# An MLP stage in another order: loads, the first token tile and the transposes rearranged

## The chip, the cores and the metric

The kernel runs on one core of a Trainium2 chip. The metric is the device time of one execution in microseconds (us). A profile of one execution gives a span from the first to the last instruction, 1.7 to 2.3 us shorter than that time in the runs here. Engines: PE is TensorE (PEld its weight loads), DVE is VectorE, ACT is ScalarE, POOL is GpSimd, SP is SyncE, which issues the DMAs. "Clock" is the TensorE clock that was granted, as a share of full speed.

## The reference

A layer norm of x (2048 tokens, 640 features) feeds two branches that are added to x: linear attention with 32 heads, and an MLP of width 1536. The MLP stage below is its first product with the gelu.

```python
xn = _layernorm(x)
return x + _A_ref(xn, A_wqkv, A_wo) + _B_ref(xn, B_w1, B_b1, B_w2, B_b2)
# _B_ref: h = gelu(xn @ w1 + b1);  h @ w2 + b2
```

## The kernel before

Tokens come in 16 tiles of 128. Each is normalized on DVE with token rows on partitions. The first MLP product needs it transposed (`xnT`), either by five PE transposes and a copy from PSUM on DVE, or by a DMA transpose issued on SP. W1 comes in four pieces of three unit columns each (`JQ = 3`, twelve units in all).

```python
dma_x(0, 1); b1 load; dma_w1(0); dma_x(1, 1); dma_w1(1); dma_x(2, 1)   # condensed
dma_w1(2); dma_x(3, 1); dma_w1(3); then x4-7, x8-11, x12-15
TD = 6                                     # tiles from 6 on are transposed by DMA
...
def h_unit(t0, n, jb):                     # one unit: 5 matmuls of n*128 columns, one gelu
    b = take(1)
    Pl.ins("tensor", [... matmul(bank(b, 0, w), W1[:, k, jb...], xnT[:, k, tok]) for k in range(DT)],
           reads=[r_W1[...]] + r_xnT[t0:t0 + n], writes=[B_[b]])
    Pl.ins("scalar", ... ACT.Gelu_apprx_tanh ...)
...
def ln_aggr(t):                            # mean and variance on DVE, then rstd on POOL
    Pl.ins(v, ... bn_aggr ...)
    Pl.ins(g, ... veps = var + EPS ...)
    Pl.ins(g, ... rstd = veps ** -0.5 ...)
def ln_norm(t):                            # on DVE, needs aggr and rstd
    ...
```

A planner writes each engine's instructions in program order and adds a wait wherever a value comes from another engine or a DMA. An instruction that waits therefore holds everything behind it on its engine. In the stage with DMA transposes the kernel before normalizes tile t - 1 after the statistics of tile t, puts one weight load after every second transpose, and two mask instructions on POOL after each tile.

## Time and profile before

| What | Value |
|---|---|
| time, median of 3 executions | 219.55 us (219.39 to 219.61) |
| span of the profiled execution | 217.9 us, clock 1.00 |
| PE busy | 208.8 us, 96% |
| first MLP matmul / first K matmul (end of the MLP stage) | 7.41 us / 64.97 us |
| waits of PE in that stage | 1.3 us for the copy of tile 1, 1.6 us for the DMA transpose of tile 11 |

How to read it: PE is nearly always busy, so the time is PE's work plus its gaps. All the work behind the MLP stage is a fixed chain, 217.9 - 64.97 = 152.9 us long. What counts is when the MLP stage ends.

This is the view of busy time in given stretches, for the kernel before; the columns are the stretch, its length, busy us and instructions of PE, PEld, DVE, ACT and POOL, then clock, DMA share and GB/s.

```profile
9.50:12.50 3.00, 1.70 (x28) 1.53 (x29) 2.44 (x7) 0.92 (x4) 0.97 (x3) 1.00 1.08 346
12.50:15.50 3.00, 3.00 (x38) 2.76 (x36) 1.86 (x6) 2.40 (x7) 0.61 (x2) 1.00 1.07 362
```

PE waits in the first stretch, and works at full clock in the second.

### The profile page before, as it was taken

The page shows a single profiled execution, that of the slowest core. Times are in us where ns is not written, and L with a number is a line of the kernel's source. Part 1 is how long each engine was busy: PE and PEld are TensorE (multiplying, and loading weights), DVE is VectorE, ACT ScalarE, POOL GpSimd, SP SyncE. Part 2 cuts the span into 40 slices and gives each one's busy share as a digit, 9 for nine tenths or more (in the row PEclk, how much of TensorE's full clock was granted, in tenths as well). Part 3 has the DMA queues.
Part 4 walks back from the last instruction along what each step waited for, and adds up shares of the span by engine and source line. Part 5 has one row for each costly group of instructions (what it writes and reads, how often), then busy time and mean ns, then how long its engine had stood idle before and what let it go on. Part 6 is the DMA issues. An engine that isn't in the chain of part 4 may idle for free.

```text
span 217.9 us, 3898 instructions
## 1 busy us (share of the span) xinstructions
PE 208.8 (96%) x1592; PEld 142.3 (65%) x1592; DVE 122.0 (56%) x217; ACT 74.2 (34%) x140; POOL 41.7 (19%) x74
## 2 busy tenths in 40 slices
PE   7799998899999999999999799999999999999994
PEld 2489987444447777777666555667767776777772
DVE  2765997000005888899168679989739316712211
ACT  2378988466667555111253653400000000000000
POOL 2221798000000000000000000099991000000000
PEclk9999999999999999999999999999999999999999
DMA  5990289995000000000000000344500110000011
GB/s 149 339 353 8 35 220 240 293 312 200 3 0 0 0 3 0 0 3 0 0 3 0 2 3 0 120 127 136 191 33 30 48 45 30 30 30 33 30 55 37
DMA packets 20425, 17.12 MB, mean 79 GB/s; under 512 B 7352, under 2 KB 20408, under 8 KB 20408
## 3 DMA queue, kind: packets, MB, share of 16 engines
q1 hardware_dynamic: 20408, 16.88, 26.2%
q8 instruction: 12, 0.20, 0.4%
q14 instruction: 5, 0.04, 0.1%
HBM read 12.62 MB, written 2.62 MB: 70 GB/s over the span
## 4 chain that ended last, share of the span: by engine, by line
PE 74%; DVE 16%; DMA 5%; SPq 1%; issue 1%; ACT 0%; DVEq 0%
PE ps L577 34%; PE ps L352 16%; PE ps L464 10%; PE ps L453 10%; DVE PQ L443 5%; DVE stats L309 4%; DMA xPK<-in_A_x_dram 3%; DMA xnT<-xn_tm 3%; PE ps L533 2%; DVE ek L441 2%; DVE rden L538 2%; DVE xn_tm L329 1%; DVE PQ L540 1%; SPq L235 1%; DVE aggr L314 1%
## 5 line engine op out<-in xcount | busy, mean ns | idle before, releaser
L352 PE MATMUL ps<-xnT,W 128*128 128x128 bf16 (+2 forms) x450 | 53.5, 280 | 3.2 <-DMA xnT<-xn_tm 1.6
L577 PE MATMUL ps<-W,HG 128*128 128x320 bf16 x384 | 54.9, 299 | 0.3 <-DVE PQ L443 0.3
L352 PEld LDWEIGHTS ps<-xnT,W 128*128 128x128 bf16 x450 | 36.3, 98 | 19.5 <-issue 2.5
L577 PEld LDWEIGHTS ps<-W,HG 128*128 128x128 bf16 x384 | 37.5, 98 | 15.7 <-issue 0.7
L356 ACT ACTIVATE HG<-ps,b1c 128x128 bf16<-128x128 f32 (+2 forms) x90 | 41.0, 489 | 17.7 <-PE ps L352 15.8
L549 POOL TENSOR_TENSOR xnT<-xnT,b2bc 128x640 bf16<-128x640 bf16 x16 | 22.6, 1451 | 104.0 <-DMA xnT<-in_A_x_dram 104.0
L440 ACT ACTIVATE ek<-ps 128x512 bf16<-128x512 f32 (+1 forms) x36 | 23.2, 645 | 23.7 <-PE ps L453 9.2
L441 DVE TENSOR_SCALAR ek<-ek 128x512 bf16<-128x512 bf16 (+1 forms) x36 | 10.9, 304 | 36.2 <-ACT ek L440 35.1
L583 DVE TENSOR_TENSOR out_sb<-ps,xnT 128x640 bf16<-128x640 f32 x15 | 12.3, 822 | 33.5 <-PE ps L577 31.5
L577 PE MATMUL ps<-Msb,PQ 128*128 128x320 bf16 x160 | 24.5, 299 | 0.0
L486 PE MATMUL ps<-xnT,Wqkv 128*128 128x512 bf16 x100 | 22.1, 379 | 0.0
L453 PE MATMUL ps<-Wqkv,xnT 128*128 128x320 bf16 x160 | 21.9, 299 | 0.0
L464 PE MATMUL ps<-xPK,xn_tm 128*128 128x320 bf16 x160 | 21.9, 299 | 0.0
L453 PEld LDWEIGHTS ps<-Wqkv,xnT 128*128 128x128 bf16 x160 | 15.7, 98 | 6.2
L464 PEld LDWEIGHTS ps<-xPK,xn_tm 128*128 128x128 bf16 x160 | 15.7, 98 | 6.1
L577 PEld LDWEIGHTS ps<-Msb,PQ 128*128 128x128 bf16 x160 | 15.7, 98 | 6.1
L309 DVE BATCH_NORM_STATS2 stats<-xPK 128x6 f32<-128x320 bf16 x32 | 15.6, 486 | 4.8 <-DMA xPK<-in_A_x_dram 4.4
L486 PEld LDWEIGHTS ps<-xnT,Wqkv 128*128 128x128 bf16 x100 | 11.7, 117 | 9.5
L443 DVE SCALAR_TENSOR_TENSOR PQ<-ps,ek 128x512 bf16<-128x512 f32 x20 | 13.8, 692 | 2.1
L443 DVE SCALAR_TENSOR_TENSOR xPK<-ps,ek 128x640 bf16<-128x640 f32 x16 | 13.2, 825 | 1.7
L538 DVE RECIPROCAL rden<-den_sb 128x512 bf16<-128x512 f32 x4 | 13.4, 3353 | 0.1
L540 DVE TENSOR_TENSOR PQ<-PQ,rden 128x512 bf16<-128x512 bf16 x20 | 12.2, 675 | 0.1
(50 smaller groups left out, 94.3 us busy)
## 6 DMA issues: line engine op xcount, KB each, us to landing
xnT<-in_A_x_dram SPq DMA_DIRECT2D x4, 640.0 KB, 4.1
Wqkv<-in_A_wqkv_dram SPq DMA_DIRECT2D x3, 800.0 KB, 6.6
out_dram<-out_sb SPq DMA_DIRECT2D x15, 160.0 KB, 1.8
W<-in_B_w_dram SPq DMA_DIRECT2D x4, 480.0 KB, 5.6
xPK<-in_A_x_dram SPq DMA_DIRECT2D x3, 640.0 KB, 8.5
W<-in_B_w_dram SPq DMA_DIRECT2D x1, 1920.0 KB, 10.1
Wo<-in_A_wo_dram SPq DMA_DIRECT2D x1, 800.0 KB, 5.5
xPK<-in_A_x_dram SPq DMA_DIRECT2D x4, 160.0 KB, 4.7
```

What stands on the lines that cost most here:

```text
L309: Pl.ins(v, lambda e: e.bn_stats(stats[:, s, 6 * h:6 * h + 6], x_in[:, t, h * HW:(h + 1) * HW]), reads=[r_x[t]], writes=[r_stats[s]])
L352: Pl.ins("tensor", [(lambda e, k=k: e.matmul(bank(b, 0, w), W1[:, k, jb * P:(jb + 1) * P], xnT[:, k, tok], start=(k == 0), stop=(k == DT - ...
L356: Pl.ins("scalar", lambda e: e.activation(HG[:, jb, tok], bank(b, 0, w), ACT.Gelu_apprx_tanh, bias=b1c[:, jb:jb + 1]), reads=[B_[b], r_b1c ...
L440: Pl.ins("scalar", lambda e: e.activation(e2, src, ACT.Exp), reads=br, writes=[r_ek[s]])
L441: Pl.ins(v, lambda e: e.tensor_scalar(et, et, 1.0, 1e-6, ALU.min, ALU.add), reads=[r_ek[s]], writes=[r_ek[s]])
L443: Pl.ins(v, lambda e: e.scalar_tensor_tensor(out=d2, in0=src, scalar=0.0, in1=e2, op0=ALU.max, op1=ALU.add), reads=br + [r_ek[s]], writes= ...
L453: fns.append(lambda e, k=k, h=h, b=b, t=t: e.matmul(bank(b + h, 0, HW), xnT[:, k, t * P:(t + 1) * P], Wqkv[:, k, D + h * HW:D + (h + 1) * ...
L464: Pl.ins("tensor", [(lambda e, t=t, h=h, b=b, f=f: e.matmul(bank(b + h, 0, HW), xn_tm[:, t, f * P:(f + 1) * P], PK[:, t, h * HW:(h + 1) * ...
L486: Pl.ins("tensor", [(lambda e, k=k, j=j, b=b: e.matmul(bank(b), Wqkv[:, k, j:D:DT], xnT[:, k, cc], start=(k == 0), stop=(k == DT - 1))) fo ...
L538: Pl.ins(v, lambda e: e.reciprocal(rden[:], den_sb[:]), reads=[r_den], writes=[r_rden])
L549: Pl.ins(g, lambda e: e.tensor_tensor(out=x_res[:, t, :], in0=x_res[:, t, :], in1=b2bc[:], op=ALU.add), reads=[r_xr[t // CH], r_b2], write ...
L577: return lambda e: e.matmul(bank(b + h, 0, HW), seq[i][0], seq[i][1][:, h * HW:(h + 1) * HW], start=(i == 0), stop=(i == n - 1))
```

## The change

The intent is to start PE earlier and to take its two waits away. Tile 0 goes in two column pieces, so that the first matmuls start on two fifths of it. Tiles 1 to 3 go through PE and all later ones through DMA, with no weight load between the transposes. x1 is loaded ahead of W1, W1's last piece ahead of x3, and b1 from ACT. The masks come at the end.

```diff
         dma_x(0, 1)
-        dma_w("sync", b1tmp[:], ...)
+        dma_x(1, 1)
         dma_w1(0)
-        dma_x(1, 1)
         dma_w1(1)
         dma_x(2, 1)
         dma_w1(2)
+        dma_w1(3)
         dma_x(3, 1)
-        dma_w1(3)
-        for c in range(1, NC):
+        dma_x(4, 2)
+        dma_x(6, 2)
+        for c in range(2, NC):
             dma_x(c * CH, CH)
 ...
+        ln_stats(0)
+        ln_half(1, 0); ln_half(1, 1); ln_aggr(1)
+        norm0(0, CA, r_xnA); norm0(CA, D, r_xnB)      # two pieces of tile 0
+        dA, sA, bA = transp0(0, 2, r_xnA)
+        filler(1)
+        dB, sB, bB = transp0(2, DT, r_xnB)             # copies: first on DVE, second on ACT
+        b1_step(); ln_norm(1); ln_half(2, 0)
+        h_first([0, 1, 2])
+        TD = 4
+        def pe_tile(t):
+            b = transp(t)
+            xnT_copy(t, b)
+            ln_half(t + 1, 1)
+            ln_aggr(t + 1)
+            ln_half(t + 2, 0)
+            ln_norm(t + 1)
+        pe_tile(1)
+        units(0, 1, 3, 2 * JQ)
+        units(1, 1, 0, 3)
+        pe_tile(2)
+        units(1, 1, 3, 2 * JQ)
+        units(0, 2, 2 * JQ, 3 * JQ)
+        pe_tile(3)
+        units(0, 2, 3 * JQ, JT)
+        for t in range(TD, NT):
+            if t > TD:
+                ln_norm(t)
+            ... dma_start_transpose(tile t) ...
+            if t + 1 < NT: ln_half(t + 1, 1); ln_aggr(t + 1)
+            if t + 2 < NT: ln_half(t + 2, 0)
+        Pl.records["sync"] += late                     # all late weights
+        run_masks(len(mask_jobs))
+        for (t0, n) in [(2, 1), (3, 1), (4, 2), (6, 2), (8, 4), (12, 4)]:
+            units(t0, n, 0, JT)
```

## The prediction

> **What bounds the kernel now.** I read the page first, then the waits of PE, the timeline of the first 40 us on all engines, the chain that ended last, and the landing time of single DMA issues.
>
> ```profile
> PE 208.8 (96%) x1592; PEld 142.3 (65%) x1592; DVE 122.0 (56%) x217; ACT 74.2 (34%) x140; POOL 41.7 (19%) x74
> ...
> PE   7799998899999999999999799999999999999994
> ```
>
> TensorE is busy for 96% of the 217.9 us span. The second line (40 slices) has two dips before the middle: the start, and slice 7 near 38 us. So an MLP reorder can win only idle time of PE, matmuls that vanish, or an earlier start. The waits of PE up to 72 us (total, times, longest) are small:
>
> ```profile
> PE ps L352 <- DMA xnT<-xn_tm: 1.6, 1, 1.6
> PE ps L352 <- DVE xnT L344: 1.6, 2, 1.3
> ```
>
> L352 is the first MLP matmul. The wait of 1.3 us is here in the timeline:
>
> ```profile
> 9.49 0.45 PE L336 MATMUL ps<-ident,xn_tm 128*128 128x128 bf16 x5 [0.24 <-DVE xn_tm L329]
> ...
> 10.29 0.49 DVE L309 BATCH_NORM_STATS2 stats<-xPK 128x6 f32<-128x320 bf16 x1 [0.22 <-DMA xPK<-in_A_x_dram]
> ...
> 10.71 0.47 DVE L344 COPY xnT<-ps 128x640 bf16<-128x640 bf16 x1
> ...
> 11.24 2.39 PE L352 MATMUL ps<-xnT,W 128*128 128x128 bf16 x35 [1.30 <-DVE xnT L344]
> ```
>
> The transposes of tile 1 are ready near 9.9, but VectorE, in program order, stands at the statistics of tile 3, whose x lands only at 10.24; the copy out of PSUM queues behind. The other wait is in the chain (start, us, what):
>
> ```profile
> 13.91 2.18 PE ps L352 x20
> ...
> 18.59 2.23 PE ps L352 x40
> ...
> 32.96 5.71 DMA xnT<-xn_tm
> 38.67 0.25 issue
> 38.91 26.06 PE ps L352 x120
> 64.97 21.73 PE ps L453 x160
> ```
>
> The transpose of tile 11 took 5.7 us because weight loads of 800 KB stand between the transposes; the first two, on an empty queue, took 2.9 and 2.6 us. The MLP ends at 64.97 and what follows is not touched: any change of that moment moves the end by as much. The same lines give the matmul pitch: 2.18/20 = 109 ns for 256 columns, 2.23/40 = 55.8 ns for 128, 26.06/120 = 217 ns for 512. A unit of five matmuls is thus 0.279, 0.545 or 1.086 us for one, two or four tiles.
>
> **What the Trainium skill says.** "TensorE: Matmul & The Clock Gate", section "Wait — 56ns, not 53.3ns?", gives a warm pitch of N/2.4 GHz plus 2.5 ns, 55.8 ns at 128 columns; the trace agrees. "DMA: Bandwidth & Descriptors", section "Queues, rings and completion order", says that each DMA engine consumes descriptors in ring order but that completion is not FIFO. Here the seven early loads did land in issue order (x0 3.1, W1 piece 0 5.9, x1 6.4, piece 1 7.8, x2 8.3, piece 2 9.8, x3 10.24), then the last W1 piece, issued at 4.85 and landed 6.9 us later:
>
> ```profile
> W<-in_B_w_dram SPq DMA_DIRECT2D x1, 480.0 KB, 6.9
> ```
>
> Section "Issuing engines are not separate DMA queues" of that page says that another issuing engine saves only sequencer time. So moving b1 to ScalarE brings no bandwidth; nothing before is issued there, so no trace shows it yet.
>
> **The change part by part.**
>
> *Loads.* x1 goes ahead of W1 piece 0, and W1 piece 3 ahead of x3. Bytes ahead of and with x1 fall from 0.80 to 0.32 MB: it lands near 3.6 to 4.0. But x3 now lands where the last W1 piece landed before, 4.85 + 6.9 = 11.75 at the latest; 0.25 us earlier if x1 fills part of the hole between 2.5 and 4.0 us, where the DMA moved only 84 to 124 GB/s. I take 11.5, against 10.24 before. This is the term on which the rest hangs.
>
> *Tile 0.* Both halves of tile 1's statistics stand ahead of tile 0's normalization, but that costs nothing: it waited 1.09 us for the rstd from POOL anyway. The first piece (256 columns) starts at 5.45 as before, is transposed near 5.9 and copied by VectorE near 6.3; the second follows a filler and goes through ScalarE, whose gelus took 0.37, 0.47 and 0.69 us for 128, 256 and 512 columns, so about 0.58 us for 384. Second half ready near 7.4. Three units are then done near 7.9, against 7.41 + 0.84 = 8.25: 0.3 us won here.
>
> *Tile 1.* Its copy no longer stands behind the statistics of tile 3, so the 1.3 us wait goes: its units run near 9.4, not 11.24.
>
> *Tile 2, the new wait.* The order on VectorE is copy of tile 1, second half of tile 2, its aggregate, first half of tile 3, and only then the normalization of tile 2. It therefore stands behind x3. PE has only six units and three more of tile 1 up to the transposes of tile 2, done near 10.3. They start at x3 + 0.42 (pitch from statistics to the next operation, 10.29 to 10.71) + 0.45 (normalization) + 0.1 = P = 12.47. So PE waits about 2.2 us here, and everything won at tiles 0 and 1 is absorbed. From P on:
>
> - transposes 0.28, three units of tile 1 0.84, three pair units 1.64: P + 2.76.
> - tile 3's normalization waits for its rstd. From an aggregate's start to the normalization it feeds is 1.30 us (4.15 to 5.45). Copy of tile 2 at P + 0.41, statistics 0.80, aggregate 1.33, normalization 2.61, done 3.06: PE starts at P + 3.10, so it waits 0.35.
> - transposes 0.28 and three pair units 1.64: P + 5.02.
> - 24 units of tiles 2 and 3 at 0.279 = 6.70: P + 11.72.
> - 24 pair units at 0.545 = 13.08: P + 24.80.
> - 24 four-tile units 26.06: P + 50.86 = 63.3.
>
> Two tiles fewer on PE are in that: 2 x 0.28 = 0.56 us. Masks at the end leave POOL's chain of veps and rstd undisturbed; before, VectorE had two stages of slack, now the loop normalizes right after the aggregate of the same tile with one half statistic between. Before, a tile took 1.53 us:
>
> ```profile
> 25.21 0.21 DVE L314 BATCH_NORM_AGGREGATE aggr<-stats 128x2 f32<-128x12 f32 x1
> ...
> 25.34 0.44 DVE L329 TENSOR_SCALAR xn_tm<-xPK,aggr,rstd 128x640 bf16<-128x640 bf16 x1
> ...
> 25.70 1.01 DVE L309 BATCH_NORM_STATS2 stats<-xPK 128x6 f32<-128x320 bf16 x2
> ```
>
> Now it takes normalization 0.36, half 0.53, aggregate to the next normalization 1.28: 2.17 us, slower, but it begins earlier: tile 4 at P + 5.71 = 18.2 (23.85 was the first by DMA, tile 6). With 0.5 to the issue and 2.6 to 2.9 to the landing, tile 5 is there at P + 11.1, needed at 11.72; tile 11 at P + 24.0 to 24.3, needed at 24.80; tile 15 near 45.5, needed near 50. So the 1.64 us wait at 38 goes, with about half a microsecond to spare. The weights start near 43 instead of 27: 2.4 MB of Wqkv at the 330 to 370 GB/s seen takes 7 us and is wanted at 63; b2, Wo and W2 follow by 58.
>
> The sum: 64.97 - 63.3 = 1.6 us earlier, which follows from -1.3 (tile 1) - 1.64 (tile 11) - 0.56 (transposes) - 0.3 (tile 0) + 2.2 + 0.35 (new waits) = -1.3, the difference being 0.3 us of small gaps before. 219.55 - 1.6 = 217.9.
>
> **Rivals.**
>
> *The x3 wait does not come.* If VectorE were past tile 3's statistics before PE runs dry, P would be 10.3 and the MLP would end near 61.2: 215.8. For it speaks the intent of the change; against it, the landing times, which are set by bytes, and the strict order of VectorE seen at 10.29.
>
> *The slower loop on VectorE becomes the bound.* 0.1 us more per tile uses 0.7 us by tile 11 and the margin is gone; 0.3 us more per tile costs about 1.5 us, and the time returns to 219.4. For it speaks the thin margin; against it, that POOL is freed of masks, which took 0.2 to 0.5 us each between its rstd steps.
>
> *The late weights become the wait.* They would have to take more than 20 us for what took under 17 when interleaved with transposes. I give this little; it would put the time above 220.
>
> *The b1 load behind other traffic* holds the in-order PE before its first units. A wait of under 4 us vanishes in the x3 wait.
>
> **Range and chances.** The centre is 217.9. The early end is x3 at 11.0 and smaller gaps (about 217.0), and a little for the first rival: 216.6. The late end is a used-up margin or x3 at 12.2: 219.2. Faster by 2% needs 215.16, below even the full first rival (215.8): 5%. Slower by 2% needs 223.9, where only the weights or b1 could bring it: 2%.
>
> **What would show it.** In the changed profile: PE idle for about 2 us before the transposes of tile 2, near 10.3 to 12.5, with VectorE's idle before the first half of tile 3 put down to the x DMA, and this longer than any wait for the copy out of PSUM. Transposes on DMA landing in under 3 us, at a pitch of about 2.2 us, with "POOL rstd" as what ended VectorE's idle in each. No wait of PE near 37. K stage starting near 63.3. I am wrong if PE runs through 10 to 13 us without a gap (then the time is below 217), or if the DMA wait at tile 4 or 8 is over 1 us (then it is 219 or more).

## The result

The changed kernel takes 221.03 us (median of 4: 220.35, 221.28, 221.28, 220.79), the kernel before 219.47 us in the same rounds (4 executions). The ratio is 1.0066, 95% interval 1.004 to 1.0092. Ratios here are the mean time of one kernel's fast runs over that of the other's of the same rounds, so not quite the ratio of the medians. That is within 2% of before, but slower beyond noise where 1.6 us faster was forecast, and outside the range of 216.6 to 219.2. The profiled execution is the fastest of the four (220.35 us); what made the others up to 0.9 us longer was not traced.

The page of the changed kernel (its slowest stretches are seen in the clock row, 40 slices of 5.5 us each):

```profile
PE 208.5 (95%) x1572; PEld 142.6 (65%) x1581; DVE 120.7 (55%) x216; ACT 74.7 (34%) x141; POOL 42.1 (19%) x74
...
PEclk9969999999999999999999999999999999999999
```

PE has two tiles of transposes fewer (a few other records are missing from both traces), yet is busy almost as long as before. The clock row has a 6, which it had nowhere before. The waits of PE from 7 to 66 us (total, times, longest):

```profile
PE ps L336 <- DVE xn_tm L329: 2.4, 1, 2.4
PE ps L352 <- issue: 1.1, 1, 1.1
```

L336 is the transpose of a tile on PE, L352 an MLP matmul. Both waits of the kernel before are gone, and two others have come. The first is the forecast one (the timeline of the first 48 us, all engines: start, us, engine, line, operation, and in brackets the idle time before it and what ended it):

```profile
11.61 0.49 DVE L309 BATCH_NORM_STATS2 stats<-xPK 128x6 f32<-128x320 bf16 x1 [1.91 <-DMA xPK<-in_A_x_dram]
12.02 0.43 DVE L329 TENSOR_SCALAR xn_tm<-xPK,aggr,rstd 128x640 bf16<-128x640 bf16 x1
...
12.51 0.71 PE L336 MATMUL ps<-ident,xn_tm 128*128 128x128 bf16 x5 [2.38 <-DVE xn_tm L329]
```

DVE stands at tile 3's statistics until x3 lands, 1.3 us later than before; only then may it normalize tile 2. PE is idle for 2.38 us. What was not forecast is what follows (the chain that ended last):

```profile
13.22 3.62 PE ps L352 x30
16.84 0.28 PE ps L336 x5
17.12 8.34 PE ps L352 x135
25.46 1.09 issue
26.55 13.26 PE ps L352 x120
...
65.71 21.73 PE ps L474 x160
```

The 30 matmuls of the first line are three units of one tile and three of two, 0.84 + 1.64 = 2.48 us at the pitches of before; they took 3.62. The stretches say why:

```profile
9.50:12.50 3.00, 0.62 (x12) 0.45 (x9) 1.04 (x3) 0.93 (x3) 0.79 (x2) 0.93 1.08 351
12.50:15.50 3.00, 2.99 (x25) 2.75 (x26) 1.50 (x5) 1.10 (x3) 0.79 (x2) 0.50 1.07 363
```

From 12.5 to 15.5 us PE is busy all the time, but at a clock of 0.50, and does 25 matmuls where the kernel before did 38 (in both a mix of 128 and 256 columns). The edges of the fall are seen in half-us stretches:

```profile
12.00:12.50 0.50, 0.00 (x0) 0.00 (x0) 0.45 (x2) 0.00 (x0) 0.00 (x0) 0.56 1.07 364
15.00:15.50 0.50, 0.50 (x5) 0.34 (x3) 0.04 (x1) 0.23 (x1) 0.36 (x1) 0.52 1.05 358
```

They read 0.56 and 0.52, so the clock was halved from about 12.06 to 15.48, for 3.4 us.

The other wait, "1.09 issue" at 25.46, has no name in the chain. Tile 4 and tile 5 must both have landed there. These are the DMA transposes of tile 4 (issued at 19.84) and of tile 5 (issued at 22.00), with the us from issue to landing last, from the view of DMA issues:

```profile
xnT<-xn_tm SPq DMA_TRANSPOSE x1, 2.6
xnT<-xn_tm SPq DMA_TRANSPOSE x1, 4.5
```

22.00 + 4.5 = 26.5: it is tile 5 that PE waits for. Its data moved from 23.0 to 24.2 us, as one would expect, and in the last of that time another queue appears (DMA queues from 24.0 to 24.5 us: packets, MB, share of 16 engines):

```profile
q8 instruction: 1, 0.02, 13.9%
```

13.9% of 16 engines for half a us is 1.1 us of one engine, for one packet. The only other transpose that took over 3.0 us was tile 11's, 4.2 us, issued at 34.98, with the next packet of that queue at 36.9. The other ten took 2.6 to 3.0.

In sum the MLP stage ends at 65.71 instead of 64.97, and 218.6 - 65.71 = 152.9 us follow, exactly as before.

### The profile page after: what moved, and what is told of

Read it like the earlier page. It is cut to its first block, busy times and chain, and to the rows that moved or that the text cites. A ratio compares the mean times of both kernels' runs of the same rounds, so it can differ in the third digit from the quotient of the medians.

```text
span 218.6 us, 3880 instructions
## 1 busy us (share of the span) xinstructions
PE 208.5 (95%) x1572; PEld 142.6 (65%) x1581; DVE 120.7 (55%) x216; ACT 74.7 (34%) x141; POOL 42.1 (19%) x74
## 4 chain that ended last, share of the span: by engine, by line
PE 83%; DVE 9%; DMA 3%; issue 2%; SPq 2%; DVEq 0%
PE ps L598 34%; PE ps L352 23%; PE ps L474 10%; PE ps L485 10%; DVE PQ L464 3%; DMA xPK<-in_A_x_dram 3%; PE ps L507 2%; PE ps L554 2%; DVE rden L559 2%; SPq L235 1%; DVE ek L462 1%; DVE PQ L561 1%; DVE W L531 1%; SPq L231 1%; DVE ZB L521 1%
## 5 line engine op out<-in xcount | busy, mean ns | idle before, releaser
L352 PE MATMUL ps<-xnT,W 128*128 128x128 bf16 (+2 forms) x432 | 53.3, 286 | 1.5 <-issue 1.1
L352 PEld LDWEIGHTS ps<-xnT,W 128*128 128x128 bf16 x435 | 36.6, 100 | 17.5 <-issue 1.2
L356 ACT ACTIVATE HG<-ps,b1c 128x128 bf16<-128x128 f32 (+2 forms) x87 | 40.3, 493 | 17.8 <-PE ps L352 15.9
L598 PE MATMUL ps<-Msb,PQ 128*128 128x320 bf16 x160 | 24.5, 299 | 0.0
L507 PE MATMUL ps<-xnT,Wqkv 128*128 128x512 bf16 x97 | 21.6, 379 | 0.2
L309 DVE BATCH_NORM_STATS2 stats<-xPK 128x6 f32<-128x320 bf16 x32 | 15.0, 469 | 5.0 <-DMA xPK<-in_A_x_dram 4.9
## 6 DMA issues: line engine op xcount, KB each, us to landing
W<-in_B_w_dram SPq DMA_DIRECT2D x1, 1920.0 KB, 15.5
```

The source lines that it names most:

```text
L309: Pl.ins(v, lambda e: e.bn_stats(stats[:, s, 6 * h:6 * h + 6], x_in[:, t, h * HW:(h + 1) * HW]), reads=[r_x[t]], writes=[r_stats[s]])
L352: Pl.ins("tensor", [(lambda e, k=k: e.matmul(bank(b, 0, w), W1[:, k, jb * P:(jb + 1) * P], xnT[:, k, tok], start=(k == 0), stop=(k == DT - ...
L356: Pl.ins("scalar", lambda e: e.activation(HG[:, jb, tok], bank(b, 0, w), ACT.Gelu_apprx_tanh, bias=b1c[:, jb:jb + 1]), reads=[B_[b], r_b1c ...
L507: Pl.ins("tensor", [(lambda e, k=k, j=j, b=b: e.matmul(bank(b), Wqkv[:, k, j:D:DT], xnT[:, k, cc], start=(k == 0), stop=(k == DT - 1))) fo ...
L598: return lambda e: e.matmul(bank(b + h, 0, HW), seq[i][0], seq[i][1][:, h * HW:(h + 1) * HW], start=(i == 0), stop=(i == n - 1))
```

## The experiments

Twelve kernels ran in three lots of four. The kernel before had medians of 219.59, 219.52 and 219.57 us. Its executions were at clock 1.00, except one (221.24 us) and three (221.41 to 221.52), which had a mean clock of 0.992. No trace of those exists, so where their clock fell is open. They count in the ratios, so I compare medians and give the ratio where it is needed.

### 1. x3 loaded ahead of the last W1 piece

```diff
-        dma_w1(3)
         dma_x(3, 1)
+        dma_w1(3)
```

> The changed kernel with x3 loaded ahead of the last W1 piece again. Theory (x3 sets tile 2, its wait lets the clock fall): x3 lands near 10.2 instead of 11.6, PE idles about 1 us before the transposes of tile 2 instead of 2.4, the granted clock stays at 1.0, the transposes start near 11.1, and the MLP ends between 62.0 and 63.5 instead of 65.7: 216.6 to 218.2 us. Rival (the slower DMA-transpose loop bounds the stage): tile 5 lands when it did, the wait moves there, and the time stays within 0.5 us of 221.0.

Measured: 218.74 us, ratio 0.9973 (0.995 to 0.9996), clock 1.0 in all four executions. That is 2.3 us less than the changed kernel, but above the 216.6 to 218.2 that I expected. PE's timeline:

```profile
11.54 0.45 PE L336 MATMUL ps<-ident,xn_tm 128*128 128x128 bf16 x5 [1.16 <-DVE xn_tm L329]
...
24.77 39.16 PE L352 MATMUL ps<-xnT,W 128*128 128x256 bf16 x237 [1.24 <-issue]
```

The gap before tile 2 is 1.16 us and the clock does not fall. The tile-2 part of the theory holds. The end, 63.9 us, is later than expected (62.0 to 63.5), because the wait for tile 5 stands: its transpose took 4.6 us again. So the rival was right about the second wait, though that wait is not a matter of DVE's loop alone, as experiment 5 shows.

### 2. The gap filled with empty matmuls

`filler(n)` issues n matmuls of 512 columns on a tile of zeros.

```diff
+        filler(9)
         pe_tile(2)
```

> The changed kernel with nine matmuls on the zero tile ahead of the transposes of tile 2, so that PE is busy for 1.9 of the 2.4 us in which it waits for x3; x3 and tile 2 come no earlier. Theory (the idle stretch costs twice, because the clock halves after it): granted clock 1.0 from 12 to 15.5 us, tile 2's transposes start at 12.5 as before, and the time falls by 1.0 to 1.5 us to about 219.7. Rival (the clock in the record is a symptom without cost, or falls at that time whatever PE does): no change, 221.0.

Measured: 220.16 us (219.49 to 220.22), ratio 1.0025, clock 1.0 in all four. Tile 2's transposes start at 12.77, no earlier than in the changed kernel. The 30 matmuls behind take 2.64 us in the timeline, where 3.83 were needed at the half clock, so the fall of the clock costs 1.2 us there. But only 0.9 us reached the end, a little less than the 1.0 to 1.5 expected:

```profile
12.77 0.45 PE L336 MATMUL ps<-ident,xn_tm 128*128 128x128 bf16 x5 [0.56 <-DVE xn_tm L329]
...
26.36 39.16 PE L352 MATMUL ps<-xnT,W 128*128 128x256 bf16 x237 [1.60 <-issue]
```

PE comes to tile 4 earlier and waits longer for tile 5, whose transpose took 5.0 us. In the profiled execution the MLP stage ends only 0.2 us earlier than the changed kernel's. The half clock is avoidable, and is a cost of its own; the wait behind it takes back part of what is won.

### 3. PE given other work ahead of tile 2

```diff
-        units(1, 1, 0, 3)
-        pe_tile(2)
-        units(1, 1, 3, 2 * JQ)
+        units(1, 1, 0, 2 * JQ)
         units(0, 2, 2 * JQ, 3 * JQ)
+        pe_tile(2)
+        units(0, 2, 3 * JQ, JT)
+        units(2, 1, 0, 5)
         pe_tile(3)
-        units(0, 2, 3 * JQ, JT)
+        units(2, 1, 5, JT)
```

> The changed kernel with PE's order alone changed: the last three units of tile 1 and three pair units go ahead of the transposes of tile 2, five units of tile 2 ahead of those of tile 3. Same loads, same order on VectorE. Theory (PE waits for x3 only because it has nothing else in its order): no gap at 10 to 12.5 us, no fall of the clock; but tile 5 then lands 2 us or more after PE is through with tile 3 (near 21.5), since VectorE's chain starts no earlier, so a wait of 2 to 4 us appears there, perhaps with the clock falling; MLP ends at 62.5 to 64.5, 217.2 to 219.2 us. Rival (the chain on VectorE was not near the bound): no wait at tile 4, MLP ends near 61, 215.7 us.

Measured: 219.81 us (219.57 to 219.93), clock 0.992 in all four: 0.6 us above the range that I gave. PE runs without a gap from 9.5 to 22 us, as expected. Then it stands at the pair of tiles 4 and 5 (tile 5 landed last, at 24.21), and the clock falls there instead:

```profile
24.30 40.83 PE L352 MATMUL ps<-xnT,W 128*128 128x256 bf16 x237 [2.34 <-DMA xnT<-xn_tm]
```

In the one-us stretches from 24 to 28 the clock is 0.66, 0.50, 0.50 and 0.63. The gap of 2.4 us had moved by 12 us, and took its halved clock along. Both costs belong to the gap, not to that moment of the kernel; and what PE wins by filling one gap it loses in the next if DVE's chain of normalizations starts no earlier.

### 4. The new order of loads alone, in the kernel before

```diff
         dma_x(0, 1)
         b1 load
+        dma_x(1, 1)
         dma_w1(0)
-        dma_x(1, 1)
         dma_w1(1)
         dma_x(2, 1)
         dma_w1(2)
-        dma_x(3, 1)
         dma_w1(3)
+        dma_x(3, 1); dma_x(4, 2); dma_x(6, 2)
```

> The kernel before with the new order of loads alone (x1 ahead of W1 piece 0, W1 piece 3 ahead of x3, x4 to x7 in two loads; b1 stays on SyncE). Theory: x3 at 11.6 holds the copy of tile 1 on VectorE until 12.0, PE idles 2.7 us or more from about 9.5 and the clock halves after it: 1.3 to 3 us slower than the kernel before, 220.8 to 222.5. Rival (the order of the loads is not what costs): within 0.4 us of 219.5.

Measured: 222.76 us (221.32 to 223.74), ratio 1.0145 (1.0099 to 1.019): 3.2 us slower than the kernel before, the largest effect of all, and a little beyond my range.

```profile
12.98 3.99 PE L354 MATMUL ps<-xnT,W 128*128 128x128 bf16 x35 [3.02 <-DVE xnT L346]
```

The 1.3 us wait of before has become 3.0, and 35 matmuls that took 2.39 us then take 3.99 now. The mean clock of the four executions was 0.992, 0.992, 0.985 and 0.999; the one at 0.999 is the fastest, 1.2 to 2.4 us ahead of the others. So the order of the loads is the part of the change that costs, and much of that cost is the clock.

### 5. The instruction packet moved

PE's matmuls and weight loads are 1592 + 1592 instructions in the kernel before, and its instruction queue q8 moved 12 packets of 0.20 MB together. The Trainium skill, "Runtime: NRT & Kernel Launch", section "Instruction fetch mechanics", says that an engine's instruction memory is refilled in blocks of 16 KiB, 256 instructions, through a DMA queue of its own. 3184 / 256 is 12.4, an estimate from the page's block size that counts no waits or branches: the packets of q8 fit PE's own instructions. If so, more PE instructions at the start move a packet to an earlier time, without a change elsewhere.

```diff
-        filler(10)                     # 10 matmuls of 512 columns on the zero tile
+        (42 matmuls of 128 columns on the zero tile)
```

> The changed kernel with its first ten zero matmuls of 512 columns replaced by 42 of 128 columns: the same stretch of time, but 64 more PE instructions, so what PE fetches after a fixed number of instructions comes about 1.8 us earlier. Theory (the transposes that share their data time with a 16 KB packet of the instruction queue land 2 us late): the packet moves from 24.0 to about 22.2, between the data of tiles 4 and 5; tile 5 lands in 2.6 to 3.0 us instead of 4.5, no wait at 25.5 us, MLP ends about 64.6, 219.9 us. Rival (the second transpose is late for a reason of its own): tile 5 takes 4.5 us again, 221.0.

Measured: 219.38 us (218.28 to 219.81). The packet came at 22.5 instead of 24.0, just after the data of tile 4. It was through at 23.7, when those of tile 5 (from 23.4) had just begun. The queue moved 13 packets in the whole execution instead of 12. The transpose of tile 5, issued at 22.37, landed in 2.9 us:

```profile
xnT<-xn_tm SPq DMA_TRANSPOSE x1, 2.9
```

This is PE's timeline behind tile 3's transposes:

```profile
17.33 47.50 PE L352 MATMUL ps<-xnT,W 128*128 128x256 bf16 x375
```

One unbroken line up to the end of the stage: the wait is gone, though PE's gap before tile 2 is still 2.39 us and the clock still fell in three of the four executions. The fourth, at 0.999, took 218.28 us, near the 217.9 that I had forecast.

> Both: x3 ahead of the last W1 piece, and the 42 narrow matmuls in place of the ten wide ones. Theory: the packet moves from 22.05 to about 20.3, tile 5 lands near 22.8 instead of 24.7, the 1.24 us wait at 23.5 goes, MLP ends near 62.7, 217.5 us. Rival: as with x3 ahead alone, 218.7.

With x3 ahead as well: 217.11 us (216.84 to 217.87), ratio 0.9887, clock 1.0 throughout, 1.6 us less than x3 ahead alone. It was run at another time. Tile 5 landed in 3.1 us, although the packet (20.4 to 21.3) still reached into the first 0.4 us of its data, and the same unbroken line appears:

```profile
14.73 47.50 PE L352 MATMUL ps<-xnT,W 128*128 128x256 bf16 x375
```

The rival (the second transpose is always late) falls in both. In the seven traces looked at with this loop on a queue without loads (the changed kernel, experiments 1, 2, 3, both of 5, and 7), every transpose that took over 3.5 us, from 4.0 to 5.0, had a packet of q8 in its data time or at its end: tile 5 or, where the packet came earlier, tile 4 (4.0 us in experiment 3), and a later one, tile 9 or 11. But not every transpose that met a packet was late: besides tile 5 here, two took only 3.3 and 3.4. In the traces of experiments 8 and 9 one transpose took 3.7 us although its packet ended 0.1 us after its issue. Why the packet holds up a transpose by about 2 us, when its own time is 1.1 us, these traces do not show.

### 6. Weights between the transposes again

```diff
             ... dma_start_transpose(tile t) ...
+            if t % 2 and late:
+                Pl.records["sync"].append(late.pop(0))
```

> The changed kernel with the late weights put between the transposes again, one load after every odd tile, as in the kernel before. Theory (the emptied queue removed the wait for tile 11): transposes behind 800 KB land in 4 to 7 us, tile 11 issued near 35 lands near 40.5 to 41.5 and PE waits 0.7 to 1.7 us for it near 40: about 222. Rival (the margin is there anyway): no such wait, 221.0.

Measured: 221.16 us (220.96 to 221.73), no different from the changed kernel by the median, and below the 222 expected. In the profile the expected wait is there:

```profile
40.17 26.06 PE L352 MATMUL ps<-xnT,W 128*128 128x512 bf16 x120 [0.83 <-DMA xnT<-xn_tm]
```

Transposes behind a large load took 3.1 to 5.6 us. So the emptied queue does remove 0.8 us of wait in this execution. It can't be read from the medians alone, since the clock falls in some executions and not in others: 220.96 and 220.97 at 1.000, 221.73 and 221.36 at 0.992. In the profiled execution the gap before tile 2 was 2.42 us, and the clock did not fall.

### 7. Masks between the tiles again

```diff
             if t + 2 < NT:
                 ln_half(t + 2, 0)
+            run_masks(2)
```

> The changed kernel with two mask instructions after each tile's part of the DMA-transpose loop. Theory: POOL is idle 1.29 us per tile in that loop and the two masks take about 0.8, so they fit: loop pitch stays 2.16 us, within 0.4 us of 221.0. Rival (masks at the end are what keeps the rstd chain short): pitch over 2.4 us, tile 11 late, 222 or more.

Measured: 220.16 us, but in two groups: 219.27 and 219.59 at clock 1.000, 220.74 and 221.36 at 0.991 and 0.992. The median misses my 0.4 us, and the reason is not the masks. DVE's loop stays at 2.16 us per tile (normalizations start at 20.55, 22.71, 24.87), so the masks fit into POOL's idle time and their place is worth nothing. The profiled execution, at clock 1.0, shows what the changed kernel does when the clock holds:

```profile
12.50 0.45 PE L336 MATMUL ps<-ident,xn_tm 128*128 128x128 bf16 x5 [2.39 <-DVE xn_tm L329]
12.79 2.64 PE L352 MATMUL ps<-xnT,W 128*128 128x128 bf16 x30
15.70 0.45 PE L336 MATMUL ps<-ident,xn_tm 128*128 128x128 bf16 x5 [0.27 <-DVE xn_tm L329]
```

It has the same gap of 2.39 us, and then 30 matmuls at full rate. Tile 3's transposes start at 15.70 instead of 16.84: between these two traces the fall costs 1.1 us. The means of the two groups differ by 1.6 us, those of the two groups of experiment 6 by only 0.6, so the cost in an untraced execution is known only roughly. The fall is a matter of the execution: the gap makes it possible, not certain.

What decides can be read from the kept traces, after the fact. Each lists the moments at which the granted clock changed (the views show only its share). In all fourteen, every stretch at full clock lasts a whole multiple of 3.413 us until the next fall (6.83 in the changed kernel, 17.07 in experiment 3, 211.6 in the kernel before), and each half-clock stretch of the MLP stage lasts one. So the changes lie on a grid of 3.413 us, and the grid's offset differs by execution: the first change to full clock comes between 4.22 and 7.26 us. I counted PE's busy time in each window of this grid from that change on. Six windows held only 0.54 to 1.25 us of it (four in the MLP stage, two at a kernel's very end), and the clock fell after each; all others held 1.71 us or more, and it fell after none. In the changed kernel one window, up to 12.06, held most of the gap and 1.25 us of work. Here a grid line at 11.05 cut the same gap in two, and the windows held 2.28 and 1.97 us. No run placed a gap on the grid on purpose, so this is a reading of traces, not a test.

### 8. Tile 0 in one piece

On the kernel with x3 ahead and the moved packet:

```diff
-        norm0 in two pieces, two groups of transposes, copies on DVE and ACT, h_first([0, 1, 2])
+        ln_norm(0); b0 = transp(0); filler(1); xnT_copy(0, b0)
+        for jb in range(3):
+            h_unit(0, 1, jb)
```

> The kernel with x3 ahead and the 42 narrow matmuls (217.1 us), with tile 0 in one piece again: one normalization, five transposes, one copy on VectorE. Theory (the start of tile 0 is absorbed by the wait before tile 2's transposes, 1.15 us there): tile 0's first units start 0.3 to 0.6 us later, that wait shrinks by as much, and the time stays within 0.3 us of 217.1. Rival (the two pieces are worth what they win at the start): 0.3 to 0.6 us slower.

Measured: 217.37 us (217.04 to 217.6, 6 executions), 0.26 us above the version in two pieces. It was run at another time. The first MLP matmul is at 7.06 instead of 6.42, 0.64 us later. The wait before tile 2's transposes did not shrink; it is 1.15 us in both. What shrank is the wait for the copy of tile 1 (0.33 us, gone), and x2 happened to land 0.24 us later in this execution, which moved tile 2 by that much. Most of the earlier start is absorbed, as the theory says. Whether 0.2 us of it survive can't be settled from these runs.

### 9. Versions meant to be faster

All three have x3 ahead, PE's order from experiment 3 with tiles 2 and 3 transposed together, and DVE's order of the kernel before (a tile is normalized after the next tile's statistics).

```diff
+        pe_copy(1); ln_half(2, 1); ln_aggr(2); ln_stats(3); ln_norm(2); ln_norm(3)
+        units(0, 1, 3, 2 * JQ); units(1, 1, 0, 2 * JQ); units(0, 2, 2 * JQ, 3 * JQ)
+        pe_copy(2, 3)                            # transposes of both, then both copies
+        units(0, 2, 3 * JQ, JT); units(2, 1, 0, JT)
+        ln_stats(4); ln_stats(5); ln_norm(4); dmaT(4)
+        for t in range(6, NT):
+            ln_stats(t); ln_norm(t - 1); dmaT(t - 1)
+        ln_norm(NT - 1); dmaT(NT - 1)
```

> A version of my own: x3 ahead of the last W1 piece; PE gets the other units of tile 1 and three pair units ahead of the transposes of tiles 2 and 3; VectorE normalizes a tile one stage after its statistics, as the kernel before did, so the loop takes 1.53 us per tile instead of 2.16. Theory: no PE wait until tile 3 is through, near 21.5; but the instruction packet comes about 1.5 us before that, near 20, in tile 5's data, so tile 5 lands near 22.8 and PE waits about 1.2 us; MLP ends near 61.9, 216.4 us. Rival (VectorE's earlier loop is enough): no wait, MLP ends at 60.6, 215.2 us.

Measured: 216.77 us (216.34 to 217.11). Tile 5 hit the packet (4.3 us for the transpose issued at 18.3) and PE waited 0.68 us; I had expected 1.2, and 216.4 us.

> The same with the 42 narrow matmuls: the packet comes about 1.8 us earlier, near 18.3, and hits tile 4, which has time. Theory: tile 4 lands near 20.7, tile 5 near 21, no wait at 21.5, MLP ends at 60.6 to 61.0, 215.2 to 215.6 us, about 1 us below the version without. Rival: no difference between the two.

Measured: 215.97 us (215.56 to 216.09), ratio 0.9811 (0.9771 to 0.9851); by the medians 215.97 / 219.57 is 1.6% faster than the kernel before: beyond noise, while whether it reaches 2% is unclear. It is 0.8 us below the version without, and 0.4 above the range that I gave. Tile 4 took 4.4 us, tile 5 3.4 us, and PE does not wait for either. Its timeline behind tile 3's transposes:

```profile
13.85 47.50 PE L352 MATMUL ps<-xnT,W 128*128 128x256 bf16 x372
```

What is left of PE's waits between the first unit and the end of the stage is 0.4 + 0.2 us. It is the fastest kernel, ahead of the kernel before and of the changed one.

> The same order as the first of the two, but tiles 4 and 5 transposed on PE like 1 to 3 (six tiles on PE, as in the kernel before). Theory: 0.56 us more matmul time, but the first DMA transpose is needed 6.5 us later, so no packet can make PE wait: MLP ends at 61.2 to 61.5, 215.8 to 216.2 us, between the other two. Rival (transposes on DMA are worth having at tiles 4 and 5 in any case): slower than both.

Measured: 216.29 us (216.13 to 216.53), between the other two, as expected, though 0.1 us above the range: two more tiles on PE cost 0.56 us of matmul time (twice the 0.28 us of five transposes) and need no luck with the packet.

## Why the prediction was wrong

Point by point, with the profiled execution, whose stage ended at 65.71 instead of the 63.3 forecast:

- **x3 and the start of tile 2.** Right. I took x3 at 11.5 and tile 2's transposes at 12.47; they were at 11.6 and 12.51. The named wait came, 2.38 us against "about 2.2 us", and it swallowed what tiles 0 and 1 won.
- **"From P on".** Wrong, and the first step that failed. The prediction laid PE's units behind the gap at the pitches of before (0.279 and 0.545 us) and put tile 3's transposes at P + 3.10. They started at 16.84, which is P + 4.33. The gap made the clock fall to half for 3.4 us. Experiment 2 (same gap, filled: no fall, 1.2 us faster there), experiment 3 (gap moved: fall moved) and the trace of experiment 7 (same gap, no fall: P + 3.20) show it. So 1.13 of the 1.23 us are the clock, and 0.10 are a wait for tile 3's rstd that was put too short. The rest of that sum was right: from tile 3's transposes to the end of tile 3's units 8.62 us were forecast and 25.46 - 16.84 = 8.62 measured.
- **"With 0.5 to the issue and 2.6 to 2.9 to the landing".** Wrong for tile 5, which took 4.5 us, and this turned a margin of 0.6 us into a wait of 1.09. The figure came from the two first transposes of the kernel before. It holds for ten of twelve. The transposes that share their time with a 16 KB packet of the instruction queue took about 2 us more; experiment 5 moved the packet, and the wait went. The sign that the prediction had named for this, a DMA wait of over 1 us at tile 4 and 219 us or more, came.
- **The loop on DVE.** Right: 2.17 us per tile forecast, 2.16 measured, ended each time by POOL's rstd. The wait for tile 11 went, with a transpose of 4.2 us in it. The prediction put the 5.7 us of before down to weight loads alone; a packet of q8 (35.4 to 36.5 us) fell into its time too. Experiment 6 shows that the loads matter.
- **Late weights, masks, b1.** Right in that none of them set the end. Weights between the transposes would have brought a wait of 0.83 us; masks are worth nothing.
- **The rivals.** I feared a bound on DVE's loop, and a margin used up at tile 11. The margin was used up at tile 5, by one late landing.

Sum: 1.23 (clock, with the 0.10) + 1.09 (tile 5) + 0.04 (P) = 2.4 us, from 63.3 to 65.7. That is the profiled execution, 220.35 us. Without the fall the changed kernel takes about 219.4 (experiment 7, two executions at clock 1.0), level with the kernel before; without the late tile 5 either, 218.3 (experiment 5, the execution at 0.999), near the forecast of 217.9. Both failures are of one kind: durations read in a stretch where PE never rested for 2 us and no packet met a transpose were carried to a stretch where both happen.

What stays open: whether a gap placed on purpose across a line of the clock's grid would be spared, why a packet of 1.1 us delays a transpose by about 2 us, and where the clock fell in the four slower executions of the kernel before.

## What to carry to other kernels

Charge a pause of TensorE of 2 us or more twice in a forecast: once as itself, and once for the half-clock stretch that may follow, 1.1 us between the two traces with the same gap and 0.6 to 1.6 between groups of executions. In the six kernels whose trace shows a gap of 2.3 us or more in the MLP stage, the mean clock says that it followed in 18 of 24 executions. A load order that holds one tile back can cost far more than its bytes suggest. A DMA transpose that is needed within half a us of its usual landing has no margin, since the fetch of PE's own instructions can add 2 us; give it a tile's time, or put that tile on TensorE. When the first fix of an in-order kernel moves a gap instead of closing it, look at the engine that feeds the gap (here the chain of normalizations on VectorE), and start that earlier.

## What the Trainium skill lacked or had wrong

- "TensorE: Matmul & The Clock Gate", section "What's actually happening", gives an idle window of about 3.4 us as what brings the half clock back. Here the half clock came at 12.06 us with PE busy for 1.25 us of the 3.4 us before (8.65 to 8.89 and 9.11 to 10.12), so a window a third full was enough (experiment 7 has the other traces: 0.54 to 1.25 us of work brought it, 1.71 us did not). It lasted 3.42 us, which agrees with the window's length. Gaps of 2.34 to 3.0 us brought it in some executions and not in others, one of 1.15 to 1.16 us in none of 14 (experiments 1, 5 with x3 ahead, and 8).
- "DMA: Bandwidth & Descriptors", section "Rules for kernel authors", says that a transpose next to ordinary DMAs needs nothing. For correctness no run contradicts it. For time it lacks that in the traces with this loop transposes of 128 x 640 took 2.6 to 3.4 us to land on a queue without loads, 3.1 to 5.6 behind large weight loads and mostly 4.0 to 5.0 beside a 16 KB instruction packet.
- "Runtime: NRT & Kernel Launch", section "Instruction fetch mechanics", calls the cost of crossing a 16 KiB boundary mostly hidden. PE itself shows no stall at the packets, which agrees; but moving one packet away from a transpose took 1.6 us off the kernel (218.74 in experiment 1, 217.11 in experiment 5).
- No page has it that the granted clock in the profile reads 1.00 in the first 5 us of the changed kernel, where ten matmuls of 512 columns took 4.28 us, 428 ns each, about twice the 217 ns of the later ones. Its list of clock changes begins only at 5.24 us, and the time before counts as full: that row shows the later fall, but not the slow start.
